# Twenty-four constant products in TensorE's early waits, and an order table drawn anew

## The chip, the cores and the metric

The kernel runs on one core of one Trainium2 chip. The metric is the device time of one execution in microseconds (us); lower is better.

The core has five engines that run side by side, each through its own list of instructions, strictly in order: TensorE (PE, matrix products), VectorE (DVE), ScalarE (ACT), GpSimd (POOL) and SyncE (SP, which here only starts DMA transfers). POOL starts some DMA transfers too. An instruction whose input isn't there yet holds up everything behind it on its engine.

## The reference

Inputs q, k and v have the shape (4 batches, 8 heads, 768 positions, 64). Attention picks, for each query, six chunks of 32 keys, by an upper bound on the scores; then a gated feed-forward layer follows.

```python
k_min = np.min(k_chunks, axis=3); k_max = np.max(k_chunks, axis=3)      # 24 chunks of 32 keys
ub = np.sum(np.maximum(q * k_min, q * k_max), axis=-1)                   # for each query and chunk
ub = np.where(causal, ub, -1e9)
top_chunks = np.argsort(ub, axis=-1)[..., -6:]
scores = scale * np.matmul(q, k.transpose(0, 1, 3, 2))
scores = np.where(mask, scores, -1e9)            # chunk among the six, and key not behind the query
attn = softmax(scores)
x = np.matmul(attn, v)                           # to 3072 tokens x 512
gate = 1 / (1 + np.exp(-(x @ w_gate)))           # 512 x 1536
out = (gate * (x @ w_val)) @ w_out               # 1536 x 512
```

## The kernel before

The 3072 tokens are 24 blocks of 128. They are worked on in eight **units** of three blocks, u0 to u7. u0 holds the first block of batches 0 to 2, for which no chunk has to be chosen; u1 holds blocks 1 to 3 of batch 0, u2 blocks 4 and 5 of batch 0 and the first block of batch 3, and so on. In a unit, keys and queries are turned (transposed), the chunks are chosen, scores, exponents and attention outputs are formed head by head, and then the feed-forward layer runs over the unit's 384 tokens. Units 4 and 5, and 6 and 7, share their feed-forward products in pairs, by a scheme with seven products for eight.

The code is a planner's. Each step of the work is added once with its name, the engines that may do it, what it reads and writes, and a function that emits its instructions. Nothing of this order reaches the chip. That is set by a written-out table, the string `ORDER`: its words are step names, in the order of emission, with the engine behind an `@` where it isn't the step's first choice, and the numbers of the buffer slots that the step opens behind a colon. Since each engine runs its instructions in order, the table is the schedule of all five engines and of both DMA-issuing queues.

```python
for word in ORDER.split():
    name, _, slots = word.partition(":")
    name, _, engine = name.partition("@")
    op = ops.pop(name)
    op.engine = engine or next(iter(op.engines))
    fresh = [b for b in op.bufs if b.slot is None]
    ...
```

PSUM, TensorE's output memory, is cut into eight slots of one kind, `ps0` to `ps7`; every product, score and transpose opens one of them.

Steps named in what follows (u is a unit, b a batch, the last number a pair of heads, a half or a block of features):

- Loads on SP: `k0_u1` to `k3_u1`, `q0_u1` to `q3_u1` (192 KB each), the same for u2 (128 KB each), `kf0_b`, `kf1_b`, `qf0_b`, `qf1_b` (halves of keys and queries of a batch's first block, 128 KB each), `vf_b` (256 KB), `v_0_1` and the like (values of one block, 256 KB).
- Weight loads on POOL: `wg0` to `wg2`, `wv0` to `wv2`, `wo0` to `wo2`, thirds of the three weights. They stand behind `after0` and `after1`, one-element copies that read a loaded query half (batch 1 and batch 2), so that the weights don't start before those loads have landed.
- u0: `kfT_b`, `qfT_b` (transposes of four pairs of heads, L598), `kf16_b`, `qf16_b` (casts), `scm_b` (two 512-column products that put the causal mask into the score banks, L642), `scf_b` (scores, L637), `expf_b_e` (exponents, L650), `vc_b` (cast of the values), `pvf_b_e` (times the values, L660), `rzf`, `xf` (normalisation), `xpsf_b_e` and `xTf_b_e` (turned output, L675, and its copy out of PSUM).
- u1 and u2: `kn`, `qn` (copies into transposing order), `kT`, `qT` (transposes, L695), `kt`, `hk0`, `hk1` (keys for the scores), `qf`, `qm`, `hq0`, `hq1` (queries), `kx0`, `kx1`, `kcr` (smallest and largest key of a chunk), `ub` (the upper bounds, L796), then `ubn`, `mx`, `ap`, `apt`, `hqm` (the choice, as a mask among the query rows). `hkp...` are copies of a constant mask pattern, `epat`, into key rows.
- Scores and outputs: `sc_u_h_y` (L857), `exp` (L868), `cm` (causal mask), `pv` (L890), `xps`, `xT`.
- Feed-forward: `g_u_f` and `v_u_f` (four 384-column products each, L940), `tanh`, `hg`, `o0`, `o1`, `o2` (L971), `osb` and `out` (eviction, L980 and L981, and store).

At the start, u0's attention and the preparation of u1 and u2 run into each other on all engines while the loads come in; the first feed-forward product, `g_u0_0`, needs all of u0's `xTf` and `wg0`, and `v_u0_0` needs `wv0`.

Of the kernel before, what the change touches and what calls it, by code (L numbers as in the profile page):

```python
# [104 lines left out]
pvf_2_0:4 kn_u2_0:5 xpsf_1_1:5 kn_u2_3:6 xTf_1_1 xpsf_1_0:3 hk1_u2_2@ACT rzf_2_1:0 rzf_2_0:1 kx1_u2_2:0 kT_u1_3:7  # L105
xTf_0_1 qT_u1_0:0 xf_2_1:1 kt_u1_3:1 kx1_u1_3 hk1_u1_3@POOL qf_u1_0 kT_u2_3:5 xTf_1_0 kT_u1_2:1 qn_u2_3@POOL:2 wv1
kx1_u1_2 wg1 kt_u1_2@DVE:0 xf_2_0:0 hk1_u1_2@ACT v11 kx0_u1_3 qT_u1_1:6 wg2 hq1_u1_0 qf_u1_1@DVE xpsf_2_1:2
qm_u1_0@ACT wv2 kx0_u1_2 kT_u2_0:3 xTf_2_1 kT_u2_1:0 kx1_u2_3 qn_u2_2@POOL:1 kx0_u2_3 wo1 kt_u2_3@DVE:2 qT_u2_3:4
kx0_u2_0 hkp100@POOL kx1_u2_0 kcr_u1 kcr1 kx0_u2_1 qn_u2_1@DVE:6 hq0 hq1 ap1 hk0_u1_2 qf_u2_3@DVE:1 xpsf_2_0:7
# [5 lines left out]
tanh_u0_5 g_u0_6:4,2,6 hq1_u1_3 hq1_u2_1@POOL hg_u0_5 v_u0_6:1 hk0_u2_3@POOL kx1_u2_1 tanh_u0_6 hq0_u1_0@POOL
kt_u2_1@DVE:0 qm_u2_0@ACT sc_u1_3_1:7,1 sc_u1_1_1:2,2 ap1_u1 hq1_u2_0 wo0 g_u0_7:5,3,7 apt1_u1 exp_u1_1_1 sc_u1_3_2:6
hqm1_u1_2@DVE sc_u1_0_1:4,3 qm_u2_2@POOL v_u0_7:0 exp_u1_3_2 tanh_u0_7 g_u0_8:2,1,8 hg_u0_7 kcr_u2@POOL v_u0_8:6
tanh_u0_8 v_0_2:5 sc_u1_3_0:5 hg_u0_8 exp_u1_3_0 sc_u1_0_0:0 g_u0_9:2,0,9 kt_u2_0@DVE:1 exp_u1_0_1 hg_u0_6 cm_u1_3
sc_u1_2_0:6,0 tanh_u0_9 v_u0_9:5 exp_u1_2_0 sc_u1_1_0:3 exp_u1_3_1 sc_u1_1_2:4 cm_u1_2 exp_u1_1_2 sc_u1_2_1:1
exp_u1_0_0 sc_u1_2_2:2 g_u0_10:6,3,10 v_u0_10:7 hqm1_u1_0@ACT cm_u1_0 k00_1 ub_u2:4,0 wo2 tanh_u0_10 exp_u1_2_2  # L120
qf1_3:3 exp_u1_1_0 g_u0_11:6,1,11 ubn0_u2:0 cm_u1_1 mx0_u2:0 sc_u1_0_2:2 v_u0_11:3 v16_0_3 tanh_u0_11 exp_u1_0_2
o0_u0_0:4,0 hk0_u2_1@ACT hg_u0_11 exp_u1_2_1 v16_0_2 ap0_u2 hq1_u1_1 o1_u0_0 hq0_u2_3@POOL ubn1_u2 pv_u1_3:6 hg_u0_10
hq0_u2_0@POOL sc_u1_4_1:2,1 sc_u1_4_2:3 hg_u0_9 sc_u1_4_0:1 exp_u1_4_1 pv_u1_1:0 mx1_u2 exp_u1_4_0 pv_u1_2
sc_u1_5_1:7,2 pv_u1_0 exp_u1_4_2 rz_u1_1:0 sc_u1_5_0:5 exp_u1_5_1 rz_u1_0:1 sc_u1_7_2:2,3 qf0_3 sc_u1_6_0:1,0 x_u1_0:2
kf1_3:0 exp_u1_6_0 sc_u1_7_0:3 x_u1_1:1 k10_1 exp_u1_5_0 sc_u1_5_2:7 ap1_u2 hq1_u2_3@DVE kf0_3 exp_u1_7_0 sc_u1_6_1:0
apt0_u2:0 cm_u1_5 exp_u1_5_2 sc_u1_6_2:1 cm_u1_7 exp_u1_7_2 sc_u1_7_1:6 xps_u1_1:5,1 o2_u0_0 exp_u1_6_2 cm_u1_4
o0_u0_1:3,1 exp_u1_7_1 osb_u0_0@DVE cm_u1_6 hqm0_u2_2@ACT xps_u1_0:7 pv_u1_7:2 exp_u1_6_1 k11_1 pv_u1_5:1 pv_u1_4
out_u0_0 pv_u1_6 rz_u1_2:0 qfT_3:6 rz_u1_3:1 xT_u1_0 sc_u2_3_0:4,2 x_u1_3:0 o1_u0_1 apt1_u2 x_u1_2:1 hqm1_u2_2
xps_u1_3:0 sc_u2_3_1:7 qf16_3@DVE:0 kfT_3:2 v_0_4:2 exp_u2_3_1 o2_u0_1 vf_3:4 kf16_3:2 q01_1:1 xps_u1_2:1
sc_u2_7_0:6,1 k16_1_0@ACT:3 kx0_1_3 k16_1_3:6 xT_u1_1@ACT v_1_1:1 kt_1_3:4 o0_u0_2:7,0 xT_u1_3@ACT hq0_u2_1 kx1_1_0:1  # L130
exp_u2_3_0 scf_3:2,5,3 o1_u0_2 v16_0_4 expf_3_1:0 hqm0_u2_0@DVE xT_u1_2@ACT o2_u0_2 kx0_1_0 exp_u2_7_0 vc_3 v_1_0:5
expf_3_0 sc_u2_3_2:0 hqm1_u2_0@DVE g_u1_0:4,2,12 kt_1_0:1 exp_u2_3_2 v_0_5:3 cmf_3_0 sc_u2_7_1:5 v_u1_0:1 cmf_3_1
exp_u2_7_1 q00_1 pvf_3_0:6 hk0_1_3 sc_u2_1_1:2,3 rzf_3_0:0 xf_3_0:2 exp_u2_1_1 k16_1_2:6 kx0_1_1 tanh_u1_0
g_u1_1:0,1,13 xpsf_3_0:5,0 q11_1 pvf_3_1:6 tanh_u1_1 v_u1_1:2 hq0_u2_2@POOL osb_u0_2@DVE hk0_u2_0@ACT g_u1_2:4,3,14
k16_1_1:0 rzf_3_1:0 hg_u1_1 v_u1_2:0 tanh_u1_2 hk1_u2_0@POOL hg_u1_0 cm_u2_3 g_u1_3:7,0,15 osb_u0_1@DVE v16_1_1
v_1_3:0 v_u1_3:2 kx1_1_1 tanh_u1_3 v16_0_5 sc_u2_4_0:4,0 hk1_1_3 sc_u2_1_2:1 kt_1_1:3 g_u1_4:3,1,16 exp_u2_1_2
xTf_3_0@ACT sc_u2_1_0:7 hg_u1_2 exp_u2_4_0 v_u1_4:1 q10_1 kx1_1_3 hk1_1_1@ACT g_u1_5:5,2,17 out_u0_2 hg_u1_3 tanh_u1_4
pv_u2_3:0 v_u1_5:4 tanh_u1_5 hk1_1_0@DVE exp_u2_1_0 kx0_1_2 g_u1_6:3,3,1 cm_u2_1 sc_u2_2_0:2,2 hg_u1_4 tanh_u1_6
v_u1_6:5 kx1_1_2 exp_u2_2_0 v_1_2:2 sc_u2_2_2:7 sc_u2_2_1:1 exp_u2_2_2 g_u1_7:3,0,0 xf_3_1:0 k00_2:0 kt_1_2:2
sc_u2_4_2:2 v_1_4:4 v_u1_7:7 tanh_u1_7 exp_u2_2_1 hg_u1_5 hk0_1_2 pv_u2_1:6 hg_u1_6 sc_u2_0_0:3,3 sc_u2_0_1:1  # L140
qf0_u3_2:0 exp_u2_0_0 cm_u2_2 g_u1_8:4,1,2 hk0_1_0 qf0_u3_0 exp_u2_4_2 sc_u2_7_2:5 pv_u2_2 exp_u2_0_1 qf0_u3_1
sc_u2_0_2:3 cm_u2_0 v_u1_8:2 hk1_u2_1@ACT hg_u1_7 v16_1_0 out_u0_1 exp_u2_7_2 hk1_1_2@DVE g_u1_9:1,2,3 v16_1_3
exp_u2_0_2 k10_2 qf0_u3_3 tanh_u1_8 v_u1_9:7 tanh_u1_9 k01_2 rz_u2_1:0 qf0_u4_2:1 cm_u2_4 qm_u3_2@ACT:0 g_u1_10:5,3,4
kcr_1@POOL hg_u1_9 cm_u2_7 v_u1_10:3 qm_u3_0 hk0_1_1 tanh_u1_10 x_u2_1:1 pv_u2_0 hg_u1_10 sc_u2_5_2:4,2 sc_u2_6_0:1,3
hq0_u3_2@POOL rz_u2_0:0 exp_u2_5_2 sc_u2_5_0:7 hg_u1_8 ub_u3:5,0 hq1_u3_0@ACT hq1_u3_2 v16_1_4 k11_2 exp_u2_5_0
x_u2_0:2 sc_u2_6_1:3 qf0_u4_3 sc_u2_6_2:4 v16_1_2 ubn1_u3:0 g_u1_11:2,0,5 exp_u2_6_1 ubn0_u3 exp_u2_6_2 sc_u2_4_1:6
hq0_u3_0 v_u1_11:7 tanh_u1_11 exp_u2_6_0 ubm0_u3 qf0_u4_1 sc_u2_5_1:0 qf0_u4_0 o0_u1_0:3,0 cm_u2_6 mx0_u3:0 q00_2:1
cm_u2_5 xps_u2_1:5 o1_u1_0 hg_u1_11 xT_u2_1@ACT exp_u2_4_1 ap0_u3 xpsf_3_1:4 apt0_u3:0 exp_u2_5_1 xps_u2_0:2 o2_u1_0
ubm1_u3 xTf_3_1 xT_u2_0@ACT mx1_u3 hqm0_u3_0@ACT pv_u2_6:1 o0_u1_1:5,1 ap1_u3 osb_u1_0 apt1_u3 out_u1_0 kx0_2_1
sc_u3_1_0:7,3 hqm1_u3_2@ACT hqm1_u3_0 pv_u2_5:6 v_1_5:1 sc_u3_1_1:0 pv_u2_7 hqm0_u3_2 k16_2_3@ACT:5 kx0_2_3 q11_2  # L150
pv_u2_4 o1_u1_1 q01_2 k16_2_2:4 exp_u3_1_0 rz_u2_2:0 x_u2_2:1 exp_u3_1_1 kx0_2_0 sc_u3_0_2:4,1 cm_u3_1 sc_u3_5_1:2,0
sc_u3_1_2:3 exp_u3_5_1 sc_u3_0_0:7 o2_u1_1 exp_u3_0_2 rz_u2_3:0 x_u2_3:0 k16_2_0@ACT:0 kt_2_2:6 sc_u3_6_0:6,2
xps_u2_2:0 xps_u2_3:2 exp_u3_0_0 sc_u3_5_2:4 o0_u1_2:1,0 kt_2_3:2 exp_u3_6_0 q10_2 exp_u3_1_2 sc_u3_0_1:7 cm_u3_6
# [1078 lines left out]
```

## Time and profile before

| | |
|---|---|
| time, median of 3 runs | 291.07 us (290.22 to 291.39) |
| profiled execution | 293.76 us, span 292.1 us |
| mean granted TensorE clock over the span | 0.977 |
| TensorE (matmul) busy | 274.0 us, 94% |
| VectorE busy | 239.4 us, 82% |
| ScalarE busy | 211.0 us, 72% |
| GpSimd busy | 108.1 us, 37% |
| DMA | 32.69 MB, mean 112 GB/s |
| longest TensorE wait | 5.8 us at the start |

The span runs from the first to the last instruction, the execution's time also takes in what lies around it. PE is the row of the matrix products; a product counts as busy from its start to its modelled end, so a busy PE can still run at half clock. The granted clock is that of TensorE: 1.00 is full speed, 0.50 half. DMA shares are the mean over the core's 16 DMA engines; a share above 1 means that packets overlap. Row groups give a start, a duration, the engine, the source line, the operation with output and inputs, and how many instructions the row joins.

### The profile page before, as it was taken

What the parts mean: (1) busy time and instruction counts of PE and PEld (TensorE: products, weight loads), DVE (VectorE), ACT (ScalarE), POOL (GpSimd) and SP (SyncE); (2) the same over time, 40 slices, a digit from 0 to 9 for tenths busy, and PEclk for the clock granted to TensorE, in tenths of its full rate; (3) what the DMA queues carried; (4) which work ended last, traced back from release to release, by engine and by line L of the source; (5) the groups of instructions that cost most, each with busy time, mean ns of one, the idle gap of its engine ahead of it and who ended that gap; (6) DMA issues with size and microseconds to landing.
All of it is one profiled execution on the core that took longest, in us unless ns stands there. A gap on an engine that the chain in (4) does not pass through costs nothing.

```text
span 292.1 us, 7079 instructions
## 1 busy us (share of the span) xinstructions
PE 274.0 (94%) x2626; PEld 173.6 (59%) x2626; DVE 239.4 (82%) x653; ACT 211.0 (72%) x450; POOL 108.1 (37%) x176
## 2 busy tenths in 40 slices
...
PEclk9977599999999999999999999999999999999999
...
GB/s 170 242 272 185 210 222 171 180 172 200 214 170 165 185 207 175 187 129 169 211 2 15 61 39 38 38 1 2 1 2 0 74 72 59 16 0 2 1 72 144
DMA packets 123378, 32.69 MB, mean 112 GB/s; under 512 B 111440, under 2 KB 120400, under 8 KB 123344
## 3 DMA queue, kind: packets, MB, share of 16 engines
...
## 4 chain that ended last, share of the span: by engine, by line
PE 83%; DVE 5%; DMA 5%; SPq 4%; issue 1%; ACT 1%; POOL 1%; DVEq 0%; ACTq 0%
PE o_u L971 19%; PE sc_u L857 11%; PE v_u L940 11%; PE g_u L940 10%; PE pv_u L890 6%; DMA wv<-in_moe_w_val_dram 3%; PE sug_u6u L1049 3%; PE suv_u6u L1049 3%; PE sug_u4u L1049 3%; PE ube_u L796 3%; PE suv_u4u L1049 2%; SPq L525 2%; SPq L536 2%; PE xps_u L917 2%; PE srv_u4u L1049 1%
## 5 line engine op out<-in xcount | busy, mean ns | idle before, releaser
L868 ACT ACTIVATE att_u<-sc_u 128x512 f16<-128x512 f32 (+3 forms) x184 | 90.1, 557 | 21.0 <-PE sc_u L857 17.1
L874 POOL TENSOR_SCALAR_AFFINE_SELECT att_u<-att_u 128x384 f16<-128x384 f16 (+1 forms) x56 | 29.9, 544 | 79.6 <-ACT att_u L868 69.5
L971 PE MATMUL o_u<-wo,hg_u 128*128 128x512 f16 x216 | 54.1, 379 | 0.0
L940 PE MATMUL v_u<-xT_u,wv 128*128 128x384 f16 x192 | 40.4, 334 | 1.8 <-DMA wv<-in_moe_w_val_dram 1.8
L940 PE MATMUL g_u<-xT_u,wg 128*128 128x384 f16 x192 | 39.7, 330 | 0.0
L948 ACT ACTIVATE gate_u<-g_u 128x384 f16<-128x384 f32 x48 | 23.1, 491 | 10.5 <-PE g_u L940 10.2
L971 PEld LDWEIGHTS <-hg_u 128*128 128x128 f16 x216 | 20.0, 98 | 16.8
L952 DVE SCALAR_TENSOR_TENSOR hg_u<-gate_u,v_u 128x384 f16<-128x384 f16 x48 | 25.0, 534 | 5.3 <-PE v_u L940 3.6
L857 PE MATMUL sc_u<-hqe,hke 128*128 128x128 f16 (+2 forms) x220 | 28.0, 243 | 0.0
L857 PE MATMUL sc_u<-hqo,hko 128*128 128x128 f16 (+2 forms) x220 | 27.6, 243 | 0.1
L890 PEld LDWEIGHTS <-att_u 128*128 128x128 f16 x640 | 24.7, 97 | 4.7 <-issue 0.6
L890 PE MATMUL pv_u<-v,att_u 128*128 128x65 f16 x640 | 26.8, 193 | 0.0
L940 PEld LDWEIGHTS <-wv 128*128 128x128 f16 x192 | 18.4, 100 | 12.6 <-DMA wv<-in_moe_w_val_dram 2.1
L940 PEld LDWEIGHTS <-wg 128*128 128x128 f16 x192 | 18.2, 99 | 10.6 <-issue 1.3
L857 PEld LDWEIGHTS <-hko 128*128 128x128 f16 x220 | 16.7, 98 | 8.5 <-issue 1.7
L857 PEld LDWEIGHTS <-hke 128*128 128x128 f16 x220 | 16.9, 98 | 6.4 <-issue 0.3
L971 PE MATMUL o_u<-wo,hgp_u 128*128 128x512 f16 (+1 forms) x72 | 16.4, 370 | 0.0
L562 POOL CAST v<-v 128x512 f16<-128x512 f32 x23 | 14.9, 660 | 0.7 <-DMA v<-in_v_dram 0.3
L909 DVE TENSOR_TENSOR x_u<-pv_u,rz_u 128x384 f16<-128x384 f32 (+1 forms) x28 | 14.5, 528 | 0.4
L981 DVE TENSOR_SCALAR osb_u<-o_u 128x512 f32<-128x512 f32 x10 | 6.8, 681 | 9.8 <-PE o_u L971 9.6
L980 ACT ACTIVATE osb_u<-o_u 128x512 f32<-128x512 f32 (+1 forms) x14 | 8.1, 589 | 8.6 <-PE o_u L971 8.6
L1049 PEld LDWEIGHTS <-Sv 128*128 128x128 f16 x96 | 9.3, 98 | 6.7 <-issue 0.4
(223 smaller groups left out, 602.4 us busy)
## 6 DMA issues: line engine op xcount, KB each, us to landing
...
```

Of the source, the lines that this page charges most:

```text
L562: plan.add(f"v16_{b}_{ib}", {POOL: pool(H * D)}, lambda e: nc.gpsimd.tensor_copy(v16[b % 2][:, ib, :, 0:D], at(t)), reads=[t], writes=[("v ...
L796: nc.tensor.matmul(at(ub[e_])[32 * p:32 * p + 32, lo - u.s0:hi - u.s0], kcr[par][ROWS[e_], p, m, :], at(src)[ROWS[e_], p, lo:hi], start=(m ...
L857: nc.tensor.matmul(at(t)[:, o:o + 128 * m], hk[b % 2][e_][:, p, 128 * jb:128 * jb + 128], hq[u.side][e_][:, p, 128 * x:128 * (x + m)], sta ...
L868: plan.add(f"exp_{u.name}_{h}_{y}", {ACT: act(n)}, lambda e, t=t, att=att, b0=b0, n=n: nc.scalar.activation(at(att)[:, b0:b0 + n], at(t), ...
L874: nc.gpsimd.affine_select(out=dv, in_=dv, compare_op=ALU.is_ge, fill=0.0, base=0, pattern=[[0, u.m], [1, 128]], channel_multiplier=-1)
L890: nc.tensor.matmul(at(pv)[:, last, x, :], at(att)[:, c:c + 128], v16[b % 2][:, jb, h, :], start=(jb == 0), stop=(jb == ib))
L909: plan.add(f"x_{u.name}_{p}", {DVE: dve(u.t)}, lambda e: nc.vector.tensor_tensor(at(x_).rearrange("p a (e d) -> p e a d", e=2), at(pv)[:, ...
L940: nc.tensor.matmul(at(t), w16[:, c, 128 * fb:128 * fb + 128], at(u.xt)[:, c, :], start=(c == 0), stop=(c == 3))
L948: plan.add(f"tanh_{u.name}_{fb}", {ACT: act(T)}, lambda e, g=g, gate=gate: nc.scalar.activation(at(gate), at(g), AF.Tanh, scale=0.5), read ...
L952: plan.add(f"hg_{u.name}_{fb}", {DVE: dve(T)}, lambda e, w_=w_, gate=gate, hg=hg: nc.vector.scalar_tensor_tensor(at(hg), at(gate), 1.0, at ...
L971: nc.tensor.matmul(at(o), hgs[c][1][1]()[:, 128 * tb:128 * tb + 128], wo16[:, fc, lo:hi], start=(c == 0), stop=(c == NFB - 1))
L1049: nc.tensor.matmul(at(t), left[i](c), right[i](c), start=first and c == 0, stop=c == 1, skip_group_check=not first)
```

## The change

One constant buffer and 24 steps are added to the plan, and `ORDER` is replaced as a whole.

```diff
+    spare = ps("spare", "wm", [128, 4, 128])
+    for i in range(24):
+        plan.add(f"wm_{i}", pe(512 / 2.4 + 2.4), lambda e: nc.tensor.matmul(
+            at(spare), ident16, ident16.unsqueeze(1).to_broadcast([128, 4, 128]), start=True, stop=True),
+            reads=["ident16"], writes=[spare], prio=-2.0 + 0.1 * i)
     prepare(units[1], 0.0, 0.8)
```

Each new step multiplies the 16-bit identity with four copies of itself, 512 columns, into PSUM slot 0. Nothing reads the result. The steps need the identity alone, and slot 0 is theirs until `wm_23` is done.

The start of the table, up to the first feed-forward products, before (first) and after:

```diff
-vf1_1:0 k1_u1:0 ident q3_u1 ident16 epat0:0 kf1_0:0 tri0 epat qf0_0:1 qf1_0 kf0_0 k2_u2:1 kn_u1_1@POOL:1 hkp011@ACT
-hkp000 kf1_1:2 tri qf0_1:3 kf0_1 v10 scm_0:0,1 hkp001@POOL k3_u2 qf1_1 qfT_0:2 vf_0:4 kfT_0:3 kf0_2:5 qf16_0@DVE:2
...
-q2_u1 after0 pvf_1_0:2 kcr_f@POOL kx0_u2_2 after1 hk0_u1_0@ACT q1_u1 pvf_1_1:5 hk1_u1_0 scf_2:3 qn_u1_0:1 xpsf_0_1:6,0
-kx1_u1_0 v_0_1:4 kn_u1_3@POOL:2 hkp111@ACT hkf1@DVE wg0 rzf_1_1:0 rzf_1_0:1 xf_1_0:2 qm_u1_3:0 vf1_2:6 kx0_u1_0
-xpsf_0_0:3 wv0 vc_2@ACT xf_1_1:0 expf_2_1:2 xTf_0_0 kn_u1_2@DVE:3 expf_2_0 pvf_2_1:2 kn_u2_1:0 qn_u1_1@POOL:4
...
-xTf_2_0@ACT qn_u1_2:3 qT_u1_2:6 k01_1:0 g_u0_0:1,0,0 v_0_3:1 qf_u1_2 qm_u1_1@ACT v_u0_0:7 hq0_u1_1 g_u0_1:2,1,1
-qn_u2_0:4 qm_u1_2@ACT hq0_u1_2@POOL v_u0_1:5 tanh_u0_0 tanh_u0_1 ub_u1:6,1 qT_u2_1:2 hg_u0_1 v16_0_1 g_u0_2:4,2,2
+k3_u1:0 epat0:0 k1_u1 tri0 epat k0_u1 q1_u1 q3_u1 q2_u2:1 hkp100@POOL kf1_0:0 qf0_0:1 kn_u1_1:0 kf0_0 hkp111@ACT ident
+qf1_1:2 hkp010@POOL ident16 hkp011 wm_0:0 k2_u1 kT_u1_1:1 q3_u2 kn_u1_3@POOL:1 wm_1 q2_u1 kt_u1_1:0 wm_2 kcr0
...
+xf_0_0:0 v_0_3:4 qf16_1:5 hk1_u1_3 qn_u1_2@POOL:4 v_0_1:2 qn_u1_0@DVE:3 kt_u1_2:1 scf_1:3 kfT_2:7 vf1_2:1 expf_1_0
+kx0_u2_2 vf1_1:2 qT_u1_2:2 vc_1 hq1 kf16_2:5 qT_u1_0:1 ap0 wm_17 wv1 xf_0_1:1 qf_u1_2 pvf_1_0:3 qfT_2:7 qf_u1_0@DVE
+expf_1_1:1 v_0_2:1 scm_2:5,2 ap1 qm_u1_2@ACT qm_u1_0@POOL wm_18 qf16_2@DVE:4 hk1_u1_1@ACT pvf_1_1:1 wm_19 kcr_u1@POOL
+xpsf_0_0:4,0 qn_u2_0:3 rzf_1_1:0 wm_20 kn_u2_3@POOL:2 xf_1_1:2 scf_2:2 hkf1 kt_u2_2@DVE:0 xpsf_1_1:7 expf_2_1:3
+xpsf_0_1:1 rzf_1_0:0 xf_1_0:0 hq0_u1_2@POOL hq0_u1_0 ub_u1:6,2 kcr1 wg1 xTf_0_0@ACT vc_2@ACT qn_u2_2@POOL:4 hkp000@ACT
+kn_u2_0@DVE:5 wg2 pvf_2_1:3 wm_21 rzf_2_1:0 qT_u2_3:4 xTf_1_1 wm_22 ubn0_u1:0 hq1_u1_0@POOL xf_2_1:2 expf_2_0 ubm0_u1
+wv2 qf_u2_3@DVE hkf0@ACT pvf_2_0:7 qT_u2_0:6 hq1_u1_1@POOL rzf_2_0:0 xpsf_1_0:3 xTf_0_1@ACT xpsf_2_1:4 xf_2_0:1 wm_23
+xTf_1_0@ACT hk0_u1_2@POOL qT_u2_2:0 hq0 kn_u2_1:0 ubn1_u1 wo1 xTf_2_1@ACT xpsf_2_0:5 xTf_2_0 kT_u2_3:1 k10_1:0
+mx0_u1:0 g_u0_0:7,0,0 hk1_u1_2@POOL ap0_u1 wo0 v_u0_0:3 ubm1_u1 kt_u2_3@DVE:1 apt0_u1:0 g_u0_1:2,1,1 hq1_u2_1@POOL
+hqm0_u1_2@ACT hqm0_u1_0 v_u0_1:4 tanh_u0_1 g_u0_2:5,2,2 hk0_u1_3@POOL tanh_u0_0 hg_u0_1 qm_u2_3@POOL:0 qf_u2_2
```

Of the first loads, five of u1's eight now come first; the first-block halves of batch 0 follow. The engine is another for many of the copies, and the buffer slots and the interleaving differ throughout, to the last unit. The last product of the table is one of u7's in both; its eviction and store end it.

More of the change, by code (lines that the diff above doesn't have):

```diff
@@ L105 @@
[L105 to L109, printed above, removed]
@@ L115 @@
[L115 to L119, printed above, removed]
@@ L120 @@
[L120 to L153, printed above, removed]
-o1_u1_2 kx1_2_2:0 exp_u3_0_1 hk0_2_3 xT_u2_3@ACT exp_u3_5_2 pv_u3_1:6 kx1_2_3 xT_u2_2@ACT o2_u1_2 cm_u3_0 v_2_1:3
@@ new lines @@
+qn_u1_3:2 k2_u2 qn_u1_1@DVE:3 v10 qf1_0 qT_u1_3:2 kx0_u1_1 vf_0:3 hkp110 wm_3 after0 qf_u1_3:0 qf0_1 kx1_u1_1:0 wm_4
+tri kn_u1_0:4 kn_u1_2@POOL:5 wm_5 qn_u2_3@DVE:6 kT_u1_0:3 wm_6 kf0_1:4 kT_u1_3:4 kt_u1_0:1 kx1_u1_0 wm_7 q1_u2
+qm_u1_3@ACT:0 kfT_0:5 kx1_u1_3 kf1_1 wm_8 hk0_u1_0 wm_9 kxf0 vf_1:5 hkp101 q0_u2 v16_0_0 kf16_0@DVE:0 qf1_2:0
+hk0_u1_1@POOL kx0_u1_0 qfT_0:6 wm_10 wm_11 qf16_0:2 wm_12 scm_0:7,2 kt_u1_3:2 wm_13 scf_0:1 kT_u1_2:1 kn_u2_2@POOL:4
+kx0_u1_3 kf0_2:1 expf_0_1:2 wm_14 kT_u2_2:6 kxf1:1 kf1_2 expf_0_0 scm_1:3,4 q0_u1 hkp001 qn_u2_1:1 qT_u1_1:2 hq0_u1_3
@@ new lines @@
+pvf_0_1:5 qf0_2 rzf_0_1:0 kcr_f qf_u1_1@DVE kfT_1:7 k3_u2 kf16_1:2 qT_u2_1:2 vf_2:3 hq1_u1_3 after1 pvf_0_0:7
+hk1_u1_0@POOL wm_15 k0_u2 rzf_0_0:1 qm_u1_1@ACT kx1_u2_2:1 wg0 qf_u2_1:1 kx0_u1_2 qfT_1:2 kx1_u1_2 wv0 k1_u2 wm_16
+xf_0_0:0 v_0_3:4 qf16_1:5 hk1_u1_3 qn_u1_2@POOL:4 v_0_1:2 qn_u1_0@DVE:3 kt_u1_2:1 scf_1:3 kfT_2:7 vf1_2:1 expf_1_0
+kx0_u2_2 vf1_1:2 qT_u1_2:2 vc_1 hq1 kf16_2:5 qT_u1_0:1 ap0 wm_17 wv1 xf_0_1:1 qf_u1_2 pvf_1_0:3 qfT_2:7 qf_u1_0@DVE
+expf_1_1:1 v_0_2:1 scm_2:5,2 ap1 qm_u1_2@ACT qm_u1_0@POOL wm_18 qf16_2@DVE:4 hk1_u1_1@ACT pvf_1_1:1 wm_19 kcr_u1@POOL
```

285 lines of the change are left out of this document (159 added, 126 removed).

## The prediction

> **What bounds the kernel now.** I read the page first, then the chain that ended last, the rows of TensorE (PE), and windows laid on the places where the clock changes.
>
> ```profile
> span 292.1 us, 7079 instructions
> ...
> PEclk9977599999999999999999999999999999999999
> ```
>
> The profiled execution took 293.76 us, 1.66 around its span of 292.1. The clock row, 7.3 us a digit, is full except in digits three to five: the cold stretches lie ahead of 37 us. What PE does after that shows in one window from its third gate product to its last product:
>
> ```profile
> 37.26:288.27 251.01, 250.41 (x2454) 1.00 0.48 97
> ...
> 288.30 0.60 ACT L980 ACTIVATE osb_u<-o_u 128x512 f32<-128x512 f32 x1 [1.45 <-PE o_u L971]
> ```
>
> PE is idle for 0.60 us of 251 (first number the length, second the busy time, then granted clock, DMA share, GB/s). The body is PE-bound, and behind it stand one eviction and its store, which the new order keeps as its last two steps. So the question is when PE gets through the first 37 us.
>
> ```profile
> 28.31 0.81 PE L940 MATMUL g_u<-xT_u,wg 128*128 128x384 f16 x4
> ...
> 36.98 0.44 PE L695 MATMUL qT_u<-ident,qn_u 128*128 128x128 f32 x2
> 37.26 0.81 PE L940 MATMUL g_u<-xT_u,wg 128*128 128x384 f16 x4
> ```
> ```profile
> 13.57 3.46 DMA qf<-in_q_dram
> ...
> 20.11 0.99 POOL wg L501
> 21.15 9.69 DMA wv<-in_moe_w_val_dram
> 30.89 1.46 PE v_u L940 x4
> 32.35 1.28 PE g_u L940 x4
> 33.63 1.28 PE v_u L940 x4
> ```
>
> The first gate product (g_u0_0) ran at 28.31, its value product (v_u0_0) waited for a weight load until 30.89, and then products that take 0.65 (37.26 to 37.91 in the full-clock body) took 1.28. The third gate product began at 37.26. This is a good mark: up to it both orders hold the same PE steps. The new one has qT_u2_0 and qT_u2_2 before it, the old one kT_u2_0 and kT_u2_1, four transposes either way, and ub_u1, which the old order runs between 34.91 (the end of the last chain row) and 36.98, stands before g_u0_0 in the new one. **So the change is worth 37.26 minus the time at which the new order reaches g_u0_2**, plus whatever the body gives back.
>
> ```profile
> 5.80:9.54 3.74, 3.28 (x13) 1.00 1.00 236
> 9.54:12.95 3.41, 2.54 (x31) 1.00 1.03 247
> 12.95:16.36 3.41, 1.49 (x13) 0.99 1.00 250
> 16.36:19.78 3.42, 3.08 (x30) 0.51 0.96 266
> 19.78:23.19 3.41, 1.90 (x27) 0.99 1.06 272
> 23.19:26.60 3.41, 3.41 (x19) 0.51 1.13 164
> 26.60:30.02 3.42, 1.49 (x11) 0.99 1.20 187
> 30.02:33.43 3.41, 2.54 (x9) 0.50 1.32 210
> 33.43:36.84 3.41, 3.41 (x37) 0.51 1.43 215
> ```
> ```profile
> 5.81 1.01 PE L642 MATMUL scf<-tri,ident 128*128 128x512 f16 x2 [5.81 <-POOL tri L486]
> 6.62 1.06 PE L598 MATMUL qfT<-ident,qf 128*128 128x128 f32 x4
> ...
> 15.26 0.59 PE L642 MATMUL scf<-tri,ident 128*128 128x512 f16 x2
> 15.69 0.60 PE L598 MATMUL kfT<-ident,kf 128*128 128x128 f32 x4
> ```
>
> The clock is granted anew every 3.41 us, by how busy PE was before: 1.49, 1.90 and 1.49 busy were each followed by half clock, 3.08 and 3.41 by full. A window with 2.54 kept its state, full at 9.54 and half at 30.02. The line lies somewhere between 1.9 and 2.5 to 3 of 3.4. The first row reads 1.00 only because no grant had been recorded yet: two 512-column products took 0.81 there (6.62 minus 5.81), and 0.43 at 15.26. The second half-clock window in a row, from 30.02, is the costly one, since nothing but PE limits that stretch.
>
> The Trainium skill, TensorE: Matmul & The Clock Gate, Part 1, has the gate fall back after an idle window. The trace differs: the windows ahead of each fall were 1.49 to 1.90 busy. By that rule the changed kernel would stay at full clock from its first filled window, and g_u0_2 would come 0.7 us earlier than I take below.
>
> **The twenty-four products.** Each is 512 columns: 0.215 us at full clock (0.43 for two), 0.40 at half, so 5.2 us in all, at most 9.7. They wait for nothing but ident16, and nobody reads them. PE time ahead of g_u0_0: the busy times above up to 28.3 are 9.8 at half clock (3.28, 3.08, 3.41) and 6.7 at full, so 11.6 at full clock; ub_u1 adds about 1.1 (2.07 us mostly at half), which makes 12.9 with the odd transposes, and 18.1 with the new products. I let PE start at 6.2 for 5.81, since POOL now makes the identity behind the mask pattern and a copy of it. Until 31 that leaves 24.8 us, of which two half-clock windows take 3.4. The products fit, with 3 us to spare; what would wait there anyway hides them. In each 3.41 us they add about 0.7 to what was 1.5 to 1.9, which brings the weak windows to 2.2 to 2.6: near the line, not safely beyond it.
>
> **When does g_u0_0 come?** Two queues decide, and both change.
>
> ```profile
> 0.00:5.00 5.00, 1.00 0.52 135
> 5.00:10.00 5.00, 1.00 1.01 236
> 10.00:15.00 5.00, 1.00 1.04 254
> 15.00:20.00 5.00, 0.66 0.98 264
> ```
>
> *Weights.* POOL issues wg0 and wv0 behind step after1, which needs the first query half of batch 2 (qf1_2). On SP that load is now the 21st, it was the 18th: 3.74 MB through it. The DMA share is 1.0, so bytes set the time: 3.13 MB by 15 us, the rest at 264 GB/s until 17.3. The chain's qf load landed at 17.03, 1.2 after its 3.34 MB had passed by the same count, so qf1_2 lands at 18.5. Then one copy (0.5) and wg0's issue (0.99): wv0 is issued at 20.3, 0.9 earlier than now, and with 9.69 to landing is there at 30.0. The bound the other way is three value loads behind it instead of one, 0.5 MB or 2 us: 32.0. I take 30.0.
>
> *ScalarE (ACT).* The transposed output of the first blocks must be in place, and its last parts are now queued on ACT.
>
> ```profile
> 7.71 0.69 DVE L347 CAST qf<-qfT 128x512 f16<-128x512 f32 x1 [3.61 <-PE qfT L598]
> ...
> 14.35 0.93 POOL L349 CAST vf<-vf 128x512 f16<-128x512 f32 x1
> ...
> 17.13 1.08 ACT L650 ACTIVATE attf<-scf 128x512 f16<-128x512 f32 x2
> 18.92 1.48 ACT L345 COPY hko<-epat 64x1536 f16<-64x1536 f16 x1
> 20.43 0.62 ACT L345 CAST vf<-vf 128x512 f16<-128x512 f32 x1
> 21.92 1.02 ACT L345 COPY kn_u<-kq_u 128x256 f32<-128x256 f32 x3
> 26.22 0.50 ACT L345 CAST hqo<-qf_u 64x384 f16<-64x384 f32 x1
> 27.11 0.35 ACT L345 COPY xT_u<-xpsf 128x256 f16<-128x256 f16 x1
> ```
>
> vc_1 stands behind wv0's issue on POOL: 20.3, 0.8 for the issue, 0.5 for qn_u1_2, 0.3 for two memsets, 0.93 for itself, 22.8. PE's pvf_1_0 waits for it, and qfT_2 is queued behind that: 23.3. DVE casts it (0.69), scf_2 follows at 24.7. Then ACT in its new order: expf_2_1 0.54, hq0_u1_0 0.50, xTf_0_0 0.35, vc_2 0.62, hkp000 1.48, expf_2_0 0.54, hkf0 about 0.6, two xTf 0.70, kn_u2_1 0.34, xTf_2_1 0.35: 6.0, so 30.7, and g_u0_0 at 31.0. The mask copy hkp000, needed much later, costs 1.48 in the middle of this. v_u0_0 follows at 31.65, so the weights are hidden by 1.6 us.
>
> From 31.0 four products at 0.65 lead to g_u0_2: 33.6. PE waits some 2 us between the exponent and the last transposes, so one half-clock window may fall here, 1.7 us; I take 0.7. **g_u0_2 at 34.3, 3.0 us earlier.** Bounds: 31.9 (g_u0_0 at 29.3, as PE alone would allow, warm), so 5.4 us won; and 37.3 (weights at 32.0, then a cold stretch), nothing won.
>
> **The body.** I take no change. It can't give more than the 0.60 us of idle time above. It can lose:
>
> ```profile
> 80.00:100.00 20.00, 20.00 (x224) 12.92 (x223) 19.75 (x61) 16.16 (x33) 10.85 (x19) 1.00 0.90 171
> ```
>
> VectorE (DVE) works 19.75 of these 20 us (the third busy time; ACT's 16.16 is the fourth). A step there that comes late under the new order has no room to be made up. On the other side the new order has 495 instructions on DVE for 510 and 458 on ACT for 452, so DVE is eased and ACT, with more room, takes it. From these I allow 0.6 gained to 2 lost.
>
> **The sum.** 293.76 minus 3.0 is 290.8 for a profiled execution; the median of the runs, 291.07, lies 2.7 below the profiled time, and I carry the same 3.0 over: **288.1 us**. If unprofiled runs lose less to the half clock now, there is less to win, which is inside the range.
>
> **Rivals.** A difference of 0.5%, 1.46 us, is about what can be told from no change: faster ends at 289.6, slower begins at 292.5.
>
> *The weights or ACT come late and PE cools while it waits.* g_u0_2 at 36 to 38.5; for 37.3: 291.1. For it: three value loads share the DMA engines with wv0. Against it: wv0 is issued earlier. 0.20.
>
> *The constant products themselves stand on the path, at half clock.* If three quarters of the time before g_u0_0 is at half, 18.1 us of PE work become 31.7; with 2 us of waits left, g_u0_0 comes at 39.9, g_u0_2 at 42.5, 5.2 later: 296.3, slower. It decides when g_u0_0 passes 36.1 (38.7 less 2.6). For it: half of the time before 28 was at half clock. Against it: every window with 3.08 or more was followed by full clock, and a PE that is behind fills its windows. 0.10. The Trainium skill, same page, Part 4: PE-mode transpose, says that transposes do not count as busy for the gate; by that the prologue, mostly transposes, would stay cold, and 296.3 would be likely. The trace speaks against it: the window from 23.19 held little but transposes like these, and the next ran at full clock:
>
> ```profile
> 23.44 1.27 PE L695 MATMUL kT_u<-ident,kn_u 128*128 128x128 f32 x5
> ```
>
> *The new order loses more in the body than it wins before it,* from 4.5 us lost on: about 293.5. DVE's 19.75 of 20 speaks for it, its lighter load against. 0.08.
>
> *All goes well*: clock full, ACT ahead, 5.4 won, 285.7. 0.12.
>
> **The numbers.** The forecast holds 0.50 (286.3 to 289.8, nearly all of it faster). Faster: 0.50 and 0.12, so 0.62; same 0.20; slower 0.10 and 0.08, so 0.18. The range from 285.5 to 292.8 takes in the two middle cases and most of the good one, and leaves out the slow ones.
>
> **What would show it.** Right: v_u0_0 not waiting for wv, ACT's last xTf releasing g_u0_0 near 31, g_u0_2 near 34, the clock full at 27 to 30, and again 251 us from there to the last product. Wrong: PE busy without a break at half clock before g_u0_0, a wait on wv past 32, or idle PE in the body.

## The result, and the profile after

The changed kernel takes 303.92 us (median, 303.63 to 305.59) where the kernel before, on the same chip, takes 291.23. The ratio is 1.044, with a 95% interval of 1.037 to 1.051: 4.4% slower, where 288.1 us, 1% faster, was predicted. The profiled execution took 304.14 us.

The page of the new kernel, with its row for SP's DMA queue, and the same row of the kernel before:

```profile
span 302.4 us, 7126 instructions
PEclk9999999999999599999959999999999999999998
q1 hardware_dynamic: 118592, 27.53, 57.2%
```
```profile
q1 hardware_dynamic: 118592, 27.53, 44.2%
```

The cold digits at the start are gone, and two new ones stand in the middle of the body. The same number of packets and of megabytes kept the 16 DMA engines busy for 57.2% of a longer span, for 44.2% before.

TensorE from its third gate product to its last product, then the stretches from the gate product g_u1_11 to g_u2_0 and from g_u3_0 to g_u3_3 (start and end; length, PE busy and count, the other engines, granted clock, DMA share, GB/s):

```profile
34.88:298.60 263.72, 255.13 (x2453) 160.74 (x2451) 210.58 (x573) 194.01 (x416) 88.91 (x136) 0.97 0.62 94
...
86.45:110.43 23.98, 19.52 (x185) 12.21 (x182) 16.73 (x57) 14.01 (x30) 10.97 (x17) 0.86 1.36 162
...
146.71:158.00 11.29, 8.27 (x40) 4.64 (x38) 7.75 (x18) 6.06 (x13) 4.64 (x8) 0.70 0.84 180
```

The third gate product came at 34.88, near the 34.3 predicted. The body was 251.01 long before, with 0.60 idle; now it is 263.72 with 8.59 idle, and nearly all of that lies in the two stretches, 4.46 (23.98 less 19.52) and 3.02. Behind each the clock is at half for some 6.8 us. PE's own waits, and the chain through the two holes:

```profile
PE kfT L598 <- ACT att_u L868: 4.5, 1, 4.5
PE g_u L940 <- DVE x_u L909: 3.0, 1, 3.0
```
```profile
84.50 0.96 SPq L546
...
85.52 3.52 SPq L546
...
89.09 2.81 SPq L546
...
91.94 6.76 DMA vf<-in_v_dram
...
99.25 0.98 ACT att_u L868 x2
100.23 1.08 PE kfT L598 x4
...
141.69 8.27 DMA q<-in_q_dram
...
150.15 0.45 DVE qf_u L763
...
150.89 0.48 DVE x_u L909
...
151.42 1.46 PE g_u L940 x4
```

Both begin with a load. At 91.9 SP issues the values of batch 3's first block (vf_3), behind three loads of batch 2's keys; ACT's cast of them (vc_3) waits until 98.7, exponents are queued behind the cast, and the transposes of kf_3 wait for a PSUM slot that those must free. At 141.7 the last quarter of batch 3's q is issued; DVE's transposing copy waits for it until 150.15, and x_u4_0 is queued behind that, so a gate product waits for its PSUM slot. The median from issue to landing tells the same of all k and q loads, first after, then before:

```profile
k<-in_k_dram SPq DMA_DIRECT2D x12, 384.0 KB, 8.2
q<-in_q_dram SPq DMA_DIRECT2D x12, 384.0 KB, 8.1
```
```profile
k<-in_k_dram SPq DMA_DIRECT2D x12, 384.0 KB, 5.9
q<-in_q_dram SPq DMA_DIRECT2D x12, 384.0 KB, 5.3
```

The k and q loads consist of 128-byte packets. By the trace's packet records each took 13.0 ns in the kernel before from 60 us on, and 17 to 26 ns in the new one, by stretches of 5 us (mean of all 73,728: 13.4 and 21.2). Two theories. **A:** the new order of SP's queue puts the wrong loads first. **B:** something slows each packet, and the holes open wherever the order leaves least time.

### The profile page after: what moved, and what is told of

Its sections match the earlier page's. It is cut to its first block, busy times and chain, and to the rows that moved or that the text cites. A ratio compares the mean times of both kernels' runs of the same rounds, so it can differ in the third digit from the quotient of the medians.

```text
span 302.4 us, 7126 instructions
## 1 busy us (share of the span) xinstructions
PE 278.4 (92%) x2650; PEld 175.3 (58%) x2650; DVE 234.1 (77%) x642; ACT 215.6 (71%) x457; POOL 112.6 (37%) x180
## 3 DMA queue, kind: packets, MB, share of 16 engines
q1 hardware_dynamic: 118592, 27.53, 57.2%
## 4 chain that ended last, share of the span: by engine, by line
PE 70%; ACT 9%; DMA 7%; SPq 5%; DVE 5%; issue 2%; POOL 2%; DVEq 0%; ACTq 0%; POOLq 0%
PE o_u L971 18%; PE sc_u L857 9%; PE g_u L940 8%; PE v_u L940 8%; PE pv_u L890 5%; DMA q<-in_q_dram 3%; SPq L546 3%; PE sug_u6u L1049 3%; PE suv_u6u L1049 3%; DMA v<-in_v_dram 2%; DMA vf<-in_v_dram 2%; PE ube_u L796 2%; SPq L556 2%; ACT gate_u4u L1074 2%; PE suv_u4u L1049 2%
## 5 line engine op out<-in xcount | busy, mean ns | idle before, releaser
L868 ACT ACTIVATE att_u<-sc_u 128x512 f16<-128x512 f32 (+3 forms) x184 | 91.4, 553 | 15.8 <-PE sc_u L857 15.1
L971 PE MATMUL o_u<-wo,hg_u 128*128 128x512 f16 x216 | 55.1, 387 | 0.0
L940 PE MATMUL g_u<-xT_u,wg 128*128 128x384 f16 x192 | 40.4, 334 | 3.6 <-DVE x_u L909 3.0
L948 ACT ACTIVATE gate_u<-g_u 128x384 f16<-128x384 f32 x48 | 23.2, 490 | 14.1 <-PE g_u L940 12.9
L971 PEld LDWEIGHTS <-hg_u 128*128 128x128 f16 x216 | 20.2, 99 | 17.9 <-issue 1.3
L857 PE MATMUL sc_u<-hqe,hke 128*128 128x128 f16 (+2 forms) x220 | 29.4, 246 | 0.0
L857 PE MATMUL sc_u<-hqo,hko 128*128 128x128 f16 (+2 forms) x220 | 28.6, 251 | 0.0
L890 PE MATMUL pv_u<-v,att_u 128*128 128x65 f16 x640 | 27.5, 193 | 0.6 <-POOL v L562 0.4
L562 POOL CAST v<-v 128x512 f16<-128x512 f32 x23 | 13.9, 611 | 19.3 <-DMA v<-in_v_dram 19.0
L980 ACT ACTIVATE osb_u<-o_u 128x512 f32<-128x512 f32 (+1 forms) x16 | 9.4, 596 | 11.6 <-PE o_u L971 11.6
L570 DVE TRANSPOSE_TENSOR_REDUCE kcr<-k 128x24 f32<-128x768 f32 x12 | 11.5, 956 | 5.5 <-DMA k<-in_k_dram 5.5
L1136 PE MATMUL spare<-ident 128*128 128x512 f16 x24 | 8.8, 413 | 7.5 <-DVE ident L480 7.5
```

The lines of the kernel that those rows point to most:

```text
L562: plan.add(f"v16_{b}_{ib}", {POOL: pool(H * D)}, lambda e: nc.gpsimd.tensor_copy(v16[b % 2][:, ib, :, 0:D], at(t)), reads=[t], writes=[("v ...
L570: plan.add(f"kx{m}_{name}_{p}", {DVE: dve(size)}, lambda e, m=m, op=op: nc.vector.tensor_reduce(out=outs[m](), in_=src(), op=op, axis=AX.X ...
L857: nc.tensor.matmul(at(t)[:, o:o + 128 * m], hk[b % 2][e_][:, p, 128 * jb:128 * jb + 128], hq[u.side][e_][:, p, 128 * x:128 * (x + m)], sta ...
L868: plan.add(f"exp_{u.name}_{h}_{y}", {ACT: act(n)}, lambda e, t=t, att=att, b0=b0, n=n: nc.scalar.activation(at(att)[:, b0:b0 + n], at(t), ...
L890: nc.tensor.matmul(at(pv)[:, last, x, :], at(att)[:, c:c + 128], v16[b % 2][:, jb, h, :], start=(jb == 0), stop=(jb == ib))
L940: nc.tensor.matmul(at(t), w16[:, c, 128 * fb:128 * fb + 128], at(u.xt)[:, c, :], start=(c == 0), stop=(c == 3))
```

## Experiments: the order of the loads

Ratios below are against runs of the kernel before on the same chip, whose medians were 291.6 to 293.1 us.

*The kernel before, profiled again.*

> The kernel before, unchanged, profiled once more beside the next three. In its first profile the 128-byte packets of the k and q loads took 13.0 ns each from 70 us on, in the new kernel's 17 to 26. Theory A (the new order itself slows the transfers): 13 ns and 291 us again. Rival (the packets' time differs from chip to chip or from run to run and has nothing to do with the order): 17 ns or more here, or a spread between the two profiles of the same kernel.

289.51 us, and 13.0 ns (mean 13.3): two executions of the kernel before agree, so the packets' time belongs to the kernel. The same profile shows something on the prediction's base. Its third gate product, and its body:

```profile
33.16 0.81 PE L940 MATMUL g_u<-xT_u,wg 128*128 128x384 f16 x4
...
33.16:284.01 250.85, 250.26 (x2454) 157.98 (x2451) 215.77 (x589) 191.53 (x411) 87.33 (x137) 1.00 0.50 100
```

The mark lies at 33.16 here, at 37.26 in the execution from which the prediction was made: 4.1 us between two executions of one kernel, in the first 37 us, with bodies that agree within 0.2.

*vf_3 ahead of batch 2's keys.*

```diff
-... v_1_0:1 ... k00_2 ... k11_2 ... k10_2 ... vf_3:5 ...
+... vf_3:5 k01_2:0 v_1_0:1 ... k00_2 ... k11_2 ... k10_2 ...
```

> The new kernel with one load moved: the values of batch 3's first block (vf_3) are issued ahead of the four k loads of batch 2 and not behind them, at some 82 us for 91.9. Theory A (the loads' order on SP's queue made the first hole): the cast of vf_3 no longer waits (6.0 us in the new kernel), TensorE's 4.5 us wait for a PSUM slot before the transposes of kf_3 goes, and with it the half-clock stretch from 99.5 to 106; the first gate product of unit 2 comes at 105 to 106 for 110.4, and the time is 298 to 300. Rival (the loads are slow as a whole, and one earlier only makes the others later): k of batch 2 is then 3 us later, so are q of batch 2 and all behind it, the second hole at 148 us grows by as much, and the time stays at 302 to 305.

303.93 us (ratio 1.0365, 1.025 to 1.048; one run of four took 300.14): no gain beyond the spread. Theory A's figure is missed. PE's waits:

```profile
PE kfT L598 <- DMA kf<-in_k_dram: 3.6, 1, 3.6
PE g_u L940 <- DVE x_u L909: 2.1, 1, 2.1
```

vf_3 was there, and the same transposes now waited 3.6 us for the next late load, half of kf_3.

*The rest of batch 3's q ahead of two value loads and a store.*

```diff
-q01_3:1 ... v_2_5:5 ... q10_3 ... out_u2_0 ... q11_3 ... q00_3
+q01_3:1 ... q10_3 q11_3 q00_3 v_2_5:5 ... out_u2_0
```

> The new kernel with three loads moved: the last three parts of batch 3's q (q10, q11, q00) are issued right behind the first (q01) and no longer behind two value loads and a store. Theory A: q is whole by 145 to 147 for 149.96, DVE does not stand 3.3 us before the transpose of its second half, the gate products of unit 3 run without the 3.0 us gap at 148, and the clock stays full there: 298 to 300 us. Rival (TensorE would have waited there for something else): the gap goes to another wait and the time stays at 302 to 305.

300.56 us (1.0304, 1.026 to 1.035), 3.4 better than the new kernel and slightly short of A's range. The wait at 148 us is gone, and another stands near it:

```profile
149.71 0.81 PE L940 MATMUL v_u<-xT_u,wv 128*128 128x384 f16 x4 [3.15 <-ACT osb_u L980]
```
```profile
145.55 3.49 DMA out_dram<-osb_u
```

ACT waits to evict an output until a store behind those loads has left its buffer. What was gained is that the clock stays up there; behind the first hole, too, it falls for one grant of 3.4 us and not for two, which the move doesn't explain.

*Both moves.*

> Both moves of the two kernels before this one. Theory A (both holes come from the order of loads alone, and are independent): the two gains add up, 292 to 295 us, and with the lead of 2.4 us from the first 37 us kept perhaps 288 to 290. Rival (the loads are slow as a whole): at least one hole stays, 297 us or more.

302.99 us (1.039, 1.032 to 1.046): the gains don't add up, and the transposes of kf_3 wait 4.0 us for their load. Where a load is brought forward, another one is late. Theory A, by which the order alone makes the holes, has missed its figure three times.

## Experiments: the landing address

What else does the table set? Besides order and engines, the slots. Memory is laid out per slot, as large as the largest tile that the slot ever holds, and in the order of the pools:

```python
head = ctx.enter_context(tc.tile_pool(name="head", bufs=1))
land = ctx.enter_context(tc.tile_pool(name="land", bufs=1))
...
pools = {"ps": banks, "kx0": head, "big": land, "v": land, "osb": land, "att": land}
```

Slot 0 of the small tiles kx is the only thing in `head`. The old table puts kx of a whole batch there (4 pairs x 24 chunks x 4 bytes, 384 bytes); the new one only that of unit 1 (4 x 12 x 4, 192). So all tiles in which loads land start at byte 16,512 + 384 = 16,896 of each partition before, 66 times 256, and at 16,704 after, a multiple of 64 and of nothing larger. A 128-byte packet then always lies across a 128-byte boundary.

*One line: unused bytes in `head`.* The order of instructions isn't touched; all tiles behind `head` move by 192 bytes.

```diff
 land = ctx.enter_context(tc.tile_pool(name="land", bufs=1))
+head.tile([128, 48], F32, tag="pad", name="pad")
```

> The new kernel with one line more: 192 bytes per partition, which nothing uses, are set aside ahead of the tiles that loads land in. The order table gives the small tiles kx their slots, and slot 0 of kx is the only thing laid out ahead of those tiles: its largest tile is 384 bytes in the old table and 192 in the new one. So the landing tiles start at byte 16,896 in the kernel before, a multiple of 256, and at 16,704 in the new one, a multiple of 64 only; with the pad they start at 16,896 again. Nothing in the order of instructions changes. Theory B (the landing address makes the 128-byte packets slow, and this opens the holes): packets of 13.0 ns as in the kernel before, both holes gone, the lead of 4.4 us at the last gate product of unit 1 kept: 286 to 289 us. Rival A (the order of loads on the queue makes them): packets of 17 to 26 ns and 302 to 305 us as before the edit.

289.87 us (0.9947, 0.992 to 0.997): 14 us for one line.

```profile
span 288.2 us, 7126 instructions
PEclk9999999999999999999999999999999999999999
q1 hardware_dynamic: 118592, 27.53, 45.4%
```
```profile
35.18:284.37 249.19, 248.73 (x2453) 158.13 (x2451) 209.35 (x573) 193.63 (x416) 89.03 (x136) 1.00 0.50 100
```

Packets of 13.1 ns, no hole, full clock. Against the 263.72 of the new kernel the body is 14.53 shorter: 8.13 of that is idle time (8.59 for 0.46), 6.40 busy time (255.13 for 248.73), which is what the half clock added.

*64 bytes instead* (`head.tile([128, 16], ...)`, start 16,768 = 131 x 128):

> The same with 64 bytes set aside: the landing tiles start at byte 16,768, a multiple of 128 and not of 256. Theory B with a line of 128 bytes: packets of 13 ns, as fast as with 192. Theory B with a line of 256 bytes: the 128-byte packets still lie inside one line and take 13 ns, but the 256-byte packets of the value loads lie across two and take longer than in the kernel before; some us lost against 192. Rival A: no change, 302 to 305 us.

290.19 us (0.996, 0.993 to 0.999), the same as with 192. The 128-byte packets took 13.8 ns on average. A multiple of 128 is enough for the time. The 256-byte packets of the values took 19.9 ns, between the 19.0 with 192 bytes and the 20.7 with none, which decides little about the length of a line.

*64 bytes in the kernel before* (start 16,960, a multiple of 64 only):

> The kernel before with 64 bytes set aside in the same place: its landing tiles move from byte 16,896 to 16,960, a multiple of 64 only, as in the new kernel. Its order of instructions is the old one. Theory B: packets of 17 to 26 ns, loads that land late, TensorE waits in the body that the kernel before doesn't have, 297 to 305 us. Rival A (the old order's queue is what keeps the loads in time): 291 us, packets of 13 ns.

299.55 us (1.026, 1.021 to 1.032), 20.2 ns, and its queue at 56.8%:

```profile
q1 hardware_dynamic: 118592, 27.53, 56.8%
...
33.87:292.00 258.13, 250.94 (x2454) 157.90 (x2451) 214.80 (x589) 191.73 (x411) 88.02 (x137) 1.00 0.63 96
```

The old order pays too: 7.2 us idle in a body that had 0.6. So address and order are told apart: the address costs the old order 8 us (299.55 against a median of 291.56), the new one 14 (303.92 against 289.87; the ratios to the kernel before, 1.044 and 0.9947, say the same). In the two profiled executions the idle time hardly differs, 7.2 and 8.6 us. What the new order pays on top is the half clock, 6.40 us of busy time, where the old one's body stays at full clock. Its waits are many and short, and the longest in its body is this one, against 4.5 and 3.0 us:

```profile
PE sc_u L858 <- ACT att_u L869: 1.8, 1, 1.8
```

Why the waits gather in two holes under the new order is not settled.

*The loads alone.* No attention, no products; the kernel's four k loads of a batch, eight times, each time from another start in one tile:

> No attention and no products here, only the loads: all four 384 KB parts of one batch's k, in 128-byte packets to 128 partitions as in the kernels, into one tile, eight times over, each time only after the last has landed; then zeros and sums are stored. The tile starts at a multiple of 256 bytes, and the eight loads land at 0, 64, 32, 128, 96, 192, 0 and 64 bytes from its start. Theory B with lines of 128 bytes: the four at 64, 32, 96 and 192... that is, at 64, 32, 96, 192 and again 64, take about 1.5 times as long as the two at 0 and the one at 128. With lines of 64 bytes: 64 and 192 are as fast as 0, only 32 and 96 are slow. With lines of 256 bytes: only the one at 192 is slow. Rival A: all eight take the same.

DVE reads the tile after each load. Its rows, with the wait for the load in brackets; the starts are 0, 64, 32, 128, 96, 192, 0 and 64 bytes:

```profile
14.80 1.79 DVE L38 TENSOR_SCALAR raw<-raw 128x3136 f32<-128x3136 f32 x1 [10.14 <-DMA raw<-in_k_dram]
29.31 1.79 DVE L38 TENSOR_SCALAR raw<-raw 128x3136 f32<-128x3136 f32 x1 [12.71 <-DMA raw<-in_k_dram]
45.10 1.79 DVE L38 TENSOR_SCALAR raw<-raw 128x3136 f32<-128x3136 f32 x1 [14.00 <-DMA raw<-in_k_dram]
56.79 1.79 DVE L38 TENSOR_SCALAR raw<-raw 128x3136 f32<-128x3136 f32 x1 [9.89 <-DMA raw<-in_k_dram]
72.52 1.79 DVE L38 TENSOR_SCALAR raw<-raw 128x3136 f32<-128x3136 f32 x1 [13.94 <-DMA raw<-in_k_dram]
88.29 1.79 DVE L38 TENSOR_SCALAR raw<-raw 128x3136 f32<-128x3136 f32 x1 [13.97 <-DMA raw<-in_k_dram]
100.33 1.79 DVE L38 TENSOR_SCALAR raw<-raw 128x3136 f32<-128x3136 f32 x1 [10.25 <-DMA raw<-in_k_dram]
114.53 1.79 DVE L38 TENSOR_SCALAR raw<-raw 128x3136 f32<-128x3136 f32 x1 [12.40 <-DMA raw<-in_k_dram]
```

9.9 to 10.3 us from the starts at 0 and 128, 12.4 to 14.0 from the others; per packet 12.8 to 12.9 ns against 20.7 to 24.2. So theory B holds without any other work on the core, the factor being 1.25 to 1.4 for a whole load and 1.6 to 1.9 for a packet. Lines of 64 bytes are out, since 64 and 192 are slow. Lines of 128 and of 256 bytes are not told apart, other than was expected: a load's packets follow one another every 128 bytes in a partition, so from 0 as from 128 every second packet starts at an odd multiple of 128, and none of them lies across a 256-byte boundary; from the other starts every second one does. Nor does either length say why 64 was cheaper than 192.

The Trainium skill, DMA: Bandwidth & Descriptors, section How a descriptor splits into AXI transactions, has each transaction start at a 256-byte boundary and count the bytes ahead of the start as beats. It tells this of bytes that are fetched, and the start that was varied here is that of the landing. For the same reason as above it would have the loads from 0 and 128 cost the same, as the trace does.

## Experiments: the products

*The padded new kernel without the twenty-four products.*

```diff
-spare = ps("spare", "wm", [128, 4, 128])
-for i in range(24):
-    plan.add(f"wm_{i}", ...)
...
-wm_0:0 ... wm_23          (24 words of the table)
```

> The first of these four without the twenty-four constant products; the order table is otherwise the new one. What it tells by theory B is their own share of the gain: TensorE busy 1.5 to 1.9 us in some of the windows before 35 us, half clock behind them, g_u0_2 1 to 3 us later than with them, and 288 to 291 us. If the products do nothing there (TensorE waits for other engines anyway): the same time as with them within 0.5 us. By rival A about 304 us.

288.40 us (0.990, 0.985 to 0.994), on the same chip and in the same minutes as the 289.87 with them. The first rows of PE, with the products and without, and the first gate product of each:

```profile
7.50 0.61 PE L1137 MATMUL spare<-ident 128*128 128x512 f16 x1 [7.50 <-DVE ident L481]
7.91 0.85 PE L696 MATMUL kT_u<-ident,kn_u 128*128 128x128 f32 x3
...
32.58 0.81 PE L941 MATMUL g_u<-xT_u,wg 128*128 128x384 f16 x4 [0.25 <-DVE xT_u L348]
```
```profile
6.00 0.90 PE L696 MATMUL kT_u<-ident,kn_u 128*128 128x128 f32 x3 [6.00 <-POOL ident masks.py:199]
...
30.50 0.81 PE L941 MATMUL g_u<-xT_u,wg 128*128 128x384 f16 x4 [0.53 <-DVE xT_u L348]
```

The first product needs the half-precision identity, which DVE has ready at 7.50; the transposes behind it need the other one, ready at 6.0. The first gate product comes 2.08 later with the products, the third at 35.18 for 33.09; it had been expected 1 to 3 us earlier with them. And the clock, for which they were a cover, holds without them in this execution from its first grant at 15.6 on:

```profile
15.60:19.01 3.41, 2.30 (x22) 1.68 (x20) 2.11 (x8) 2.72 (x7) 1.62 (x4) 1.00 1.03 253
...
25.84:29.25 3.41, 1.91 (x40) 1.07 (x18) 1.90 (x8) 3.38 (x6) 3.36 (x6) 1.00 1.22 198
29.25:32.67 3.42, 2.85 (x20) 1.64 (x19) 3.14 (x18) 0.94 (x4) 3.33 (x7) 1.00 1.21 198
```

It doesn't hold in every execution. Each run has its mean granted clock on record. Without the products (these six runs, and twelve of the last kernel below) it was 0.997 or more in 8 of 18, which took 287.6 to 288.8 us; the other ten, at 0.985 to 0.994, took 288.6 to 292.0. With them (twelve runs padded with 192 bytes, ten with 64) it was 0.997 or more in 18 of 22, which took 289.4 to 290.3, and the other four, at 0.992, took 291.3 to 291.4. So the products do hold the clock more often, but where it holds either way they cost about 1.5 us.

*The first product behind the first transposes* (one word of the table, `wm_0:0`, moved behind `kT_u1_1`).

> The new kernel with 192 bytes set aside, and its first constant product moved behind the first transposes (kT_u1_1). With all products in the new kernel's places TensorE's first instruction waits until 7.50 us for the half-precision identity, which DVE copies, while those transposes need only the single-precision one, there at 6.0. Theory Q (that wait at the head of TensorE's queue is most of what the products cost): the transposes at 6.0, everything behind 1 to 1.5 us earlier, g_u0_2 at 33.9 to 34.3 for 35.18, 288.5 to 289. Rival (their own busy time is the cost): the transposes at 6.0, but g_u0_2 within 0.4 us of 35.18 and 289.9.

Transposes at 6.01, third gate product at 34.12, span 287.1 for 288.2: 1.06 of the 2.09 us. Theory Q holds for half of the cost. The chain that ended last still holds eleven of the products, on a path that PE, ACT and DVE pass in turn; the other half is put down to them, though no run takes them out alone. 289.93 us (0.990, 0.986 to 0.994): 288.8 and 289.3 in the two runs at full clock, 289.9 to 290.0 in the three at 0.992.

*The old order with the products* (three to eight at each of its early waits, on five short-lived spare tiles).

> The old order (landing tiles at a multiple of 256 as in the kernel before) with twenty-four constant products added where its TensorE waits early: three ahead of the transposes of the second query half, three ahead of those of kn_u1_0, eight ahead of the first pvf of the second blocks (its longest wait, 2.35 us), three ahead of qT_u1_1, four ahead of qT_u1_2 and three ahead of the first value product. Theory P (they keep the clock granted where the old order loses it): no half-clock window after the start, g_u0_2 at 32.5 to 34 and not at 33.2 to 37.3 as in the two profiles of the kernel before, 288.5 to 290. Rival (TensorE waits there for ACT and the weights in any case, and a product that comes at the wrong moment delays a transpose that others wait for): 291 to 293.

290.75 us (0.9962, 0.993 to 0.999). The clock is full throughout, and 0.997 or more in all twelve runs, where the kernel before never passed 0.994; the third gate product came at 35.42, no better than without, since v_u0_0 still waited 1.5 us for wv and two groups of products stood 1.4 and 0.9 us behind DVE. A gain of a fraction of 1%, between the two figures expected.

*The new order, neither pad nor products: the kx slots 0 and 1 exchanged.*

```diff
-kx1_u1_1:0 kxf1:1 kx1_u2_2:1 kx1_1_3:1 kx1_2_3:1 kx1_3_2:1
+kx1_u1_1:1 kxf1:0 kx1_u2_2:0 kx1_1_3:0 kx1_2_3:0 kx1_3_2:0
```

> The new order without the products and without any pad: in the order table the slot numbers 0 and 1 of the six kx tiles change places, so that slot 0 holds the 384-byte ones as in the old table. The landing tiles start at byte 16,896. Theory B: packets of 13 ns and 288.4 us, as with the pad, for six characters of the table. Rival (the pad did something else): about 302 us.

289.32 us (0.9914, 0.987 to 0.996), packets of 13.1 ns, third gate product at 33.11. Without the products, six characters of the table do what the pad did (0.9896). Three versions beat the kernel before by about 1%: this one, the padded one without products, and the padded one whose first product stands behind the first transposes.

## Why the prediction was wrong

- **The mark.** g_u0_2 at 34.88 for 34.3: the right size, partly by luck. The weights were hidden, as said (v_u0_0 ran at 32.93 without a wait). ACT's last copy ended at 31.80 for 30.7, and what released g_u0_0 was one on DVE behind it (xTf_2_0), so it ran at 32.28 for 31.0. PE started at 7.50, not 6.2, because the term took the time of POOL's identity and not of the copy that DVE makes of it. The 1.28 us of delay were half made up by the 0.7 taken for a half-clock window that didn't come.
- **"What would wait there anyway hides them"** was wrong. Taking the products away brought the mark forward by 2.1 us. Half of that was their own wait, at the head of an engine that runs in order.
- **The clock rule** was drawn too firmly. Laid on the windows of 3.41 us between two grants, and from the first recorded grant on, TensorE at full clock fell to half behind every window with up to 1.58 us busy and stayed up behind every one with 1.91 or more, over all the kernels here; in between both occurred (1.72 and 1.90 fell; 1.59 to 1.90 stayed in six). At half clock, 2.46 to 2.86 busy kept it there and 3.08 or more ended it. A window that stayed up in the padded kernel (first two rows), and the windows ahead of the two falls in the new one (last two):

```profile
18.72:22.13 3.41, 1.86 (x15) 1.04 (x13) 2.66 (x8) 2.24 (x5) 2.49 (x5) 1.00 0.99 215
22.13:25.55 3.42, 3.20 (x35) 2.57 (x35) 3.23 (x9) 3.24 (x8) 2.20 (x4) 1.00 1.06 163
```
```profile
95.91:99.32 3.41, 0.00 (x0) 0.00 (x0) 1.53 (x3) 0.59 (x2) 1.48 (x2) 1.00 0.99 230
...
147.11:150.52 3.41, 1.28 (x9) 0.61 (x7) 0.37 (x1) 1.92 (x4) 0.00 (x0) 1.00 0.90 153
```

  The rule of the Trainium skill that the prediction set against its own (TensorE: Matmul & The Clock Gate, Part 1: an idle window makes it fall) fits the first of these falls and not the second, ahead of which TensorE was busy for 1.28 us.
- **"The body. I take no change"** is the step that failed, by 14 us: with 0.6 gained to 2 lost allowed, the body took 263.72 us for 251.01, and 249.19 once the landing tiles lay at 16,896 again. The step asked whether DVE would be late and took the loads as they were, although the table had redrawn SP's queue and, through its slot numbers, the addresses at which every load lands. The rival of a body that loses had the sign (293.5 at 0.08), and neither size nor cause.
- **"It can't give more than the 0.60 us of idle time"** was wrong too, the other way: with aligned tiles the new order's body is 249.2 for 250.9, with 248.7 busy for 250.3. The same products keep PE busy 1.5 us less in the new sequence; why was not looked into.
- **The base.** 3.0 us were forecast, and 2.4 came, against a mark of 37.26, which belongs to a late execution; against 33.16 nothing was won. Carrying the 3.0 over to the median was a mis-sized term, and the prediction had said that there might be less to win. With the addresses mended, the whole change is worth 0.5% (289.87), and the order alone about 1%.
- **Slips in the working**, none of which moved the forecast: the load qf1_2 is the 23rd on SP and was the 19th, and the bytes counted are right for the 23rd. Of 18.1 us of PE work, 31.7 come out when three quarters of the work are at half clock; with three quarters of the time it is 29.0, and that rival 2.7 us cheaper. PE alone, warm, would reach g_u0_0 at 24.3 by the terms given (6.2 and 18.1), not at 29.3.
